# Gate functions as one activation each: x times sigmoid on ScalarE, without VectorE's multiplication

## The chip, the core and the metric

The kernel runs on one NeuronCore of one Trainium2 chip. Its engines are TensorE (PE in the profile, with PEld for its weight loads), VectorE (DVE), ScalarE (ACT), GpSimd (POOL) and SyncE (SP, which starts the DMAs). The program lists the instructions of each engine in an order of its own, and an engine that waits for an operand holds up what is listed behind it. The metric is device time in microseconds, the lower the better.

## What is computed

Chunked attention, then two feed-forward layers, all in float32. The attention output of 4608 tokens with 512 features goes through a layer with a gate and a value branch (d_ff 1536), then through one with a gate alone (d_ff 2048):

```python
def _moe_ref(x, w_gate, w_val, w_out) -> np.ndarray:
    g = x @ w_gate
    silu = g * (1.0 / (1.0 + np.exp(-g)))
    val = x @ w_val
    return (silu * val @ w_out).astype(np.float32)

def _moe2_ref(x, w_in, w_out) -> np.ndarray:
    h = x @ w_in
    g = h * (1.0 / (1.0 + np.exp(-1.702 * h)))
    return (g @ w_out).astype(np.float32)
```

## The kernel before

Matrix products run as three products of a high and a low part each (mm3, lines 249 to 251), so every operand has to be split: ACT or POOL casts the high part, DVE or POOL subtracts it from the value to get the low part (split, line 244, which calls copy and tt). Both layers use seven products for a 2x2 block of products (labels "1" to "7"), with sums and differences of the blocks made on DVE and POOL.

There are four passes over 9 blocks of 512 tokens: two over halves of layer 1's weights, two over halves of layer 2's. In the first pass, attention for the next block (attend, line 464) runs between the products; beside each pass DVE, ACT and POOL also convert the weights of the next one (conv_part, line 323).

In layer 1, group_products (line 579) makes seven products, ACT copies some of them out of PSUM and DVE adds others to them, into tiles c (gate and value beside one another). gated (line 606) then takes Sigmoid of the gate on ACT into h (line 613), multiplies h by the gate and then by the value on DVE (line 616, which is recorded as line 242), and splits h into hh and hl. second (line 623) multiplies these by the output weights.

In layer 2, group_gated (line 632) makes seven products in the order of ORDER[2], "1675243". Almost all of them go through one PSUM bank, ga: the next product waits until ACT has copied the last one out (labels "1", "6", "7", "5") or DVE has added it (labels "2", "4", "3"). gate (line 647) takes Sigmoid with scale 1.702 into a quarter of xr (line 654) and multiplies it by its argument on DVE (line 656). From the four gates of a step DVE makes the combinations (lines 706 to 713), which are split for the seven last products (last_product, line 717). Between two products of ga, PE works on last products of the step before.

The order on each engine isn't the order of the code. Program.emit (line 99) sorts the operations with a list scheduler: each operation has an estimated time (act_us, dve_us, pool_us, GV, YS, OS; 1.3 us for a change of ACT's function table), a due time and its dependences, and at each step the scheduler emits the operation that can start first by these estimates; among those that can start within 0.1 us (DVE) or 0.3 us (others) it takes the one due first. An operation that is taken away therefore changes the order on all engines after it.

Of the kernel before, what the change touches and what calls it, by code (L numbers as in the profile page):

```python
# [12 lines left out]
AF = mybir.ActivationFunctionType  # L13
ALU = mybir.AluOpType
# [55 lines left out]
class Program:  # L70
# [5 lines left out]
    def op(self, eng, us, fn, reads=(), writes=(), prio=0, table=None, near=None):  # L76
        o = Op()
        o.eng, o.us, o.fn, o.prio, o.table, o.near, o.n = eng, us, fn, prio, table, self.slack if near is None and eng not in ('pe', 'dma') else near, len(self.ops)
        deps, follows = set(), set()
        for b in reads:  # L80
            deps.update(next((a.writers for a in b.line() if a.writers), ()))
        for b in writes:
            deps.update(b.users)
            if not b.users:
                if b.prev is not None:
                    deps.update(b.prev.users)
                if b.before is not None and b.before.tile is None:
                    follows.add(b.before.users[0])
        for b in (*reads, *writes):
            for a in b.line():  # L90
                a.users.append(o)
        for b in writes:
            for a in b.line():
                a.writers.append(o)
        o.deps, o.follows = deps, follows - deps
        self.ops.append(o)
        return o
# [44 lines left out]
def attention_two_moe_kernel(ctx: ExitStack, tc: tile.TileContext, q, k, v, wg, wv, wo, wi, wo2, out):  # L142
# [25 lines left out]
    nc = tc.nc  # L168
# [16 lines left out]
    scale = 1.0 / float(D) ** 0.5  # L185
# [18 lines left out]
    op = prog.op  # L204
# [8 lines left out]
    def act_us(n):  # L213
        return (200 + n) / 1.2e3

    def dve_us(n):
        return (148 + n) / 0.96e3

    def pool_us(n):
        return (128 + n) / 0.46e3  # L220
# [10 lines left out]
    def copy(dst, src, n, prio, eng="act", cut=lambda ap: ap, near=None):  # L231
        if eng == "act":
            op("act", act_us(n), lambda: nc.scalar.copy(out=dst.ap, in_=cut(src.ap)), [src], [dst], prio, near=near)  # L233
        elif eng == "pool":
            op("pool", pool_us(0.6 * n), lambda: nc.gpsimd.tensor_copy(dst.ap, cut(src.ap)), [src], [dst], prio)  # L235
        else:
            op("dve", dve_us(n), lambda: nc.vector.tensor_copy(dst.ap, cut(src.ap)), [src], [dst], prio)

    def tt(dst, a, b, by, n, prio, eng="dve", of_a=lambda ap: ap, of_b=lambda ap: ap, near=None):
        e = nc.vector if eng == "dve" else nc.gpsimd  # L240
        op(eng, dve_us(n) if eng == "dve" else pool_us(n),
           lambda: e.tensor_tensor(out=dst.ap, in0=of_a(a.ap), in1=of_b(b.ap), op=by), [a, b], [dst], prio, near=near)  # L242

    def split(hi, lo, src, n, prio, eng="dve", cut=lambda ap: ap, hi_eng="act"):
        copy(hi, src, n, prio, hi_eng, cut)
        tt(lo, src, hi, ALU.subtract, n, prio, eng, of_a=cut, of_b=rd)
# [321 lines left out]
    def product(m, w, x, goes_on, prio, near=None):  # L568

        def fn():  # L570
            for var in range(2):
                for kk in range(2):
                    ks = slice(kk * P, kk * P + P)
                    mm3(m.ap[:, var], w.ap[:, var, 0, ks], w.ap[:, var, 1, ks], x.ap[:, 0, kk], x.ap[:, 1, kk],
                        kk == var == 0 and not goes_on, kk == 1, skip_group_check=True)

        op("pe", GV, fn, [w, x], [m], prio, near=near)
# [28 lines left out]
    def gated(g, c, prio):  # L606

        def of(var):
            return lambda ap: ap[:, :, var]

        for i in (1, 0):
            h = ring["h"].new([P, 2, HT])
            op("act", act_us(512), lambda h=h, i=i: nc.scalar.activation(  # L613
                out=h.ap, in_=of(0)(c[i].ap), func=AF.Sigmoid), [c[i]], [h], prio, "sig")
            for var in range(2):
                tt(h, h, c[i], ALU.mult, 512, prio, of_b=of(var))
            hh = ring["hh"].new([P, BT], F32R)
            hl = ring["hl"].new([P, BT], F32R)
            split(*[Buf(lambda s=s: s.ap.rearrange("p (n t) -> p n t", n=2), s.prev, s.before, s) for s in (hh, hl)],
                  h, 512, prio)  # L620
            yield i, hh, hl
# [10 lines left out]
    def group_gated(g, xs, at, put, early, apart):  # L632


        s1, u2, u3 = [ring["u"].new([P, 2, HT]) for _ in range(3)]
        made = {}
        hs = []

        quarters = []

        def quarter():
            if not quarters:
                c = ring["c"].new([P, 2, 2, HT])
                quarters.extend(c.part(lambda ap, k=k: ap[:, k]) for k in range(2))
            return quarters.pop(0)

        def gate(c, k, prio):
            if apart:
                h = ring["ttte"[k]].new([P, 2, HT])
            else:  # L650
                if not hs:
                    hs.append(ring["xr"].new([P, 4, 2, HT]))
                h = hs[0].part(lambda ap: ap[:, k])
            op("act", act_us(512), lambda: nc.scalar.activation(out=h.ap, in_=c.ap, func=AF.Sigmoid, scale=1.702),  # L654
               [c], [h], prio, "sig")
            tt(h, h, c, ALU.mult, 512, prio)
            return h

        def parts(label, src, prio, eng="dve"):
            made[label] = [ring[t].new([P, 2, HT], F32R) for t in HOMES[label]]  # L660
            split(*made[label], src, 512, prio, eng)

        def follow(label, prio):
            m = bank[label]
            if label == "1":
                copy(s1, m, 512, prio, near=0.3)
            elif label == "6":
                copy(u2, m, 512, prio, near=0.3)
            elif label == "7":
                copy(u3, m, 512, prio, near=0.3)  # L670
                tt(u2, u2, u3, ALU.subtract, 512, prio, "pool")
            elif label == "5":
                c = quarter()
                copy(c, m, 512, prio, near=0.3)
                tt(u2, u2, c, ALU.add, 512, prio, "pool")
                a["22"] = gate(c, 3, prio + 1)
                parts("4", a["22"], prio + 3, "pool")
            elif label == "2":
                c = quarter()
                tt(c, s1, m, ALU.add, 512, prio, near=0.3)  # L680
                a["11"] = gate(c, 0, prio + 1)
                parts("1", a["11"], prio + 2)
            elif label == "4":
                c = quarter()
                tt(c, u3, m, ALU.subtract, 512, prio, near=0.3)
                a["12"] = gate(c, 1, prio + 1)
                parts("2", a["12"], prio + 3)
            else:
                c = quarter()
                tt(c, u2, m, ALU.add, 512, prio, near=0.3)  # L690
                a["21"] = gate(c, 2, prio + 1)

        a = {}
        alone = {"2": "gb", "3": "s", "4": "a"} if early else {}
        z = ring["ga"].new([P, 2, HT])
        bank = {label: ring[alone[label]].new([P, 2, HT]) if label in alone else z for label in ORDER[2]}
        for i, label in enumerate("1263745" if early else ORDER[2]):
            n = ORDER[2].index(label)
            product(bank[label], W[g][n], xs[n], label in "675", at(i), 0.25)
            if label != "3" or not early:  # L700
                follow(label, at(i))
            if i == 6:
                if early:
                    follow("3", at(i))
                prio = at(i)
                tt(a["22"], a["21"], a["22"], ALU.add, 512, prio + 1)
                parts("5", a["22"], prio + 2)
                tt(a["21"], a["11"], a["21"], ALU.subtract, 512, prio + 2)
                tt(a["11"], a["22"], a["11"], ALU.subtract, 512, prio + 2)
                parts("6", a["11"], prio + 3)  # L710
                parts("7", a["21"], prio + 4)
                tt(a["12"], a["12"], a["11"], ALU.subtract, 512, prio + 4)
                parts("3", a["12"], prio + 5)
            put(i)
        return made
# [152 lines left out]
    for p, (layer, gs) in enumerate(passes):  # L868
        jobs = spread(p)
        for b in range(NB):  # L870
            t = start[p][b]
            xs = X.pop((p, b))
            for j, g in enumerate(gs):
# [10 lines left out]
                def at(i, tj=tj, step=step):  # L884
                    return tj + (i + (i > 4)) * step / 8

                if layer == 1:
                    c = group_products(g, xs, at, put, p)
# [106 lines left out]
```

## Time and profile before

| | us |
|---|---|
| median of three runs | 1773.23 |
| lowest and highest run | 1772.24, 1777.48 |
| span of the profiled execution | 1771.6 |
| PE busy | 1702.8 (96%) |
| DVE busy | 1307.8 (74%) |
| ACT busy | 878.3 (50%) |
| POOL busy | 765.7 (43%) |

The span reaches from the first to the last instruction of one profiled execution. The execution's own time isn't given apart from it; the lowest run is 0.6 us above the span, the median 1.6. Instructions are grouped by the line that records them: line 242 is tt, so DVE's multiplications, additions and subtractions all stand under it and are told apart by their tiles (h<-h,c and xr<-xr,c are the gate multiplications, c<-u,ga an addition that empties bank ga, hl<-h,hh a low part). An "idle before" of an engine is put down to the operation that released it.

### The profile page before, as it was taken

To read this page: it belongs to the slowest core of one execution; us is meant where nothing else is said; L and a number is where in the kernel's file an instruction comes from. 1 tells how busy PE (TensorE), PEld (TensorE's weight loads), DVE (VectorE), ACT (ScalarE), POOL (GpSimd) and SP (SyncE) were. 2 spreads that over 40 slices of the span, in tenths; PEclk is the share of its full clock that TensorE was granted. 3 is DMA by queue.
4 is the path that set the end of the run, shared out by engine and by line. 5 is a ranking of instruction groups with operands and counts; after the bars stand their busy time and mean duration, and the time that the engine had idled before them with its cause. 6 is when DMAs were issued, how large, how long until landed. Compare 5 with 4: busy or idle time off the path is not lost.

```text
span 1771.6 us, 36678 instructions
## 1 busy us (share of the span) xinstructions
PE 1702.8 (96%) x14392; PEld 1617.6 (91%) x14392; DVE 1307.8 (74%) x1884; ACT 878.3 (50%) x1534; POOL 765.7 (43%) x762
## 2 busy tenths in 40 slices
PE   6879999999999999999999989999999999999998
PEld 6769988989898999999999989999999999999997
DVE  6888788777876467555555659899887777777777
ACT  5766566666663344333333345555554444444442
POOL 4664456355643145422222225667563133333333
PEclk8889999999999999999999999999999999999999
DMA  6467887788778989877778997888889977776775
GB/s 249 162 220 268 280 280 256 252 300 282 251 256 316 338 280 314 291 262 255 256 250 270 362 354 257 283 273 299 283 285 312 377 264 243 245 238 215 229 224 160
DMA packets 187325, 477.93 MB, mean 270 GB/s; under 512 B 20112, under 2 KB 47760, under 8 KB 187152
## 3 DMA queue, kind: packets, MB, share of 16 engines
q1 hardware_dynamic: 187152, 475.58, 79.0%
q8 instruction: 114, 1.87, 0.4%
q14 instruction: 59, 0.48, 0.1%
HBM read 334.46 MB, written 141.03 MB: 268 GB/s over the span
## 4 chain that ended last, share of the span: by engine, by line
PE 76%; DVE 11%; DMA 5%; issue 2%; POOL 1%; ACT 1%; SPq 0%; POOLq 0%; ACTq 0%; DVEq 0%
PE ga L249 9%; PE ga L251 9%; PE ga L250 9%; PE yb L249 4%; PE ya L250 4%; PE ya L251 4%; PE ya L249 4%; PE yb L251 4%; PE yb L250 4%; PE gb L249 4%; PE gb L251 4%; PE gb L250 4%; DVE xr L242 2%; PE s L249 2%; PE s L250 2%
## 5 line engine op out<-in xcount | busy, mean ns | idle before, releaser
L249 PE MATMUL ga<-x,w 128*128 128x256 f32 x1640 | 472.3, 288 | 26.0 <-DVE c L242 12.3
L250 PE MATMUL ga<-x,w 128*128 128x256 f32 x1640 | 464.5, 283 | 3.0 <-DVE x L242 3.0
L251 PE MATMUL ga<-x,w 128*128 128x256 f32 x1640 | 464.7, 283 | 0.0
L249 PEld LDWEIGHTS ga<-x,w 128*128 128x128 f32 x1640 | 312.1, 190 | 38.5 <-ACT u L233 15.2
L250 PEld LDWEIGHTS ga<-x,w 128*128 128x128 f32 x1640 | 312.1, 190 | 7.6 <-DVE x L242 3.3
L251 PEld LDWEIGHTS ga<-x,w 128*128 128x128 f32 x1640 | 312.0, 190 | 0.0
L233 ACT COPY u<-ga 128x512 f32<-128x512 f32 x231 | 135.4, 586 | 243.9 <-PE ga L251 243.3
L242 DVE TENSOR_TENSOR c<-u,ga 128x512 f32<-128x512 f32 x143 | 97.9, 684 | 120.8 <-PE ga L251 119.8
L242 DVE TENSOR_TENSOR h<-h,c 128x512 f32<-128x512 f32 x216 | 170.6, 807 | 12.6 <-ACT h L613 10.9
L654 ACT ACTIVATE xr<-c 128x512 f32<-128x512 f32 x140 | 87.4, 631 | 139.8 <-DVE c L242 101.7
L249 PE MATMUL gb<-x,w 128*128 128x256 f32 x500 | 142.6, 285 | 2.7 <-DVE c L242 2.7
L251 PE MATMUL gb<-x,w 128*128 128x256 f32 x500 | 141.2, 282 | 0.0
L250 PE MATMUL gb<-x,w 128*128 128x256 f32 x500 | 140.8, 282 | 0.0
L242 DVE TENSOR_TENSOR xr<-xr,c 128x512 f32<-128x512 f32 x140 | 128.4, 924 | 12.9 <-ACT xr L654 12.7
L242 POOL TENSOR_TENSOR u<-u 128x512 f32<-128x512 f32 x36 | 53.9, 1498 | 189.9 <-ACT u L233 188.2
L242 DVE TENSOR_TENSOR c<-u,gb 128x512 f32<-128x512 f32 x125 | 85.3, 682 | 65.9 <-ACT u L233 42.9
L613 ACT ACTIVATE h<-c 128x512 f32<-128x512 f32 x108 | 68.1, 633 | 121.0 <-DVE c L242 120.7
L235 POOL CAST ws<-t 128x256 fp32r<-128x256 f32 x78 | 50.6, 649 | 162.2 <-DVE h L242 65.0
L242 DVE TENSOR_TENSOR xr<-xr 128x512 f32<-128x512 f32 x140 | 111.2, 794 | 1.4
L242 POOL TENSOR_TENSOR k<-xr,q 128x512 fp32r<-128x512 f32 x24 | 41.3, 1720 | 158.1 <-DVE xt L242 69.0
L235 POOL CAST ws<-st 128x256 fp32r<-128x256 f32 x88 | 51.4, 584 | 120.5 <-DMA od_b<-ws 46.8
L249 PEld LDWEIGHTS gb<-x,w 128*128 128x128 f32 x500 | 94.5, 189 | 5.8 <-DVE c L242 3.1
(255 smaller groups left out, 5175.2 us busy)
## 6 DMA issues: line engine op xcount, KB each, us to landing
x<-x_dram SPq DMA_DIRECT2D x189, 512.0 KB, 5.5
o<-od_b SPq DMA_DIRECT2D x126, 512.0 KB, 4.5
o<-od_a SPq DMA_DIRECT2D x102, 512.0 KB, 5.2
x_dram<-x SPq DMA_DIRECT2D x63, 512.0 KB, 4.6
wd_b<-ws SPq DMA_DIRECT2D x56, 256.0 KB, 4.7
od_b<-ws SPq DMA_DIRECT2D x56, 256.0 KB, 4.8
w<-wd_b SPq DMA_DIRECT2D x28, 512.0 KB, 6.4
raw<-in_moe_w_out SPq DMA_DIRECT2D x56, 255.8 KB, 4.5
```

The source lines that it names most:

```text
L233: op("act", act_us(n), lambda: nc.scalar.copy(out=dst.ap, in_=cut(src.ap)), [src], [dst], prio, near=near)
L235: op("pool", pool_us(0.6 * n), lambda: nc.gpsimd.tensor_copy(dst.ap, cut(src.ap)), [src], [dst], prio)
L242: lambda: e.tensor_tensor(out=dst.ap, in0=of_a(a.ap), in1=of_b(b.ap), op=by), [a, b], [dst], prio, near=near)
L249: nc.tensor.matmul(o, ah, bh, start=first, stop=False, **kind)
L250: nc.tensor.matmul(o, ah, bl, start=False, stop=False, **kind)
L251: nc.tensor.matmul(o, al, bh, start=False, stop=last, **kind)
L613: op("act", act_us(512), lambda h=h, i=i: nc.scalar.activation(out=h.ap, in_=of(0)(c[i].ap), func=AF.Sigmoid), [c[i]], [h], prio, "sig")
L654: op("act", act_us(512), lambda: nc.scalar.activation(out=h.ap, in_=c.ap, func=AF.Sigmoid, scale=1.702), [c], [h], prio, "sig")
```

## The change

Layer 1's gate becomes AF.Silu in one activation, and only the multiplication by the value stays. Layer 2's gate becomes AF.Gelu_apprx_sigmoid, and no multiplication stays. The names handed to the planner for the function table change too.

```diff
@@ -611,9 +611,8 @@
         for i in (1, 0):
             h = ring["h"].new([P, 2, HT])
             op("act", act_us(512), lambda h=h, i=i: nc.scalar.activation(
-                out=h.ap, in_=of(0)(c[i].ap), func=AF.Sigmoid), [c[i]], [h], prio, "sig")
-            for var in range(2):
-                tt(h, h, c[i], ALU.mult, 512, prio, of_b=of(var))
+                out=h.ap, in_=of(0)(c[i].ap), func=AF.Silu), [c[i]], [h], prio, "silu")
+            tt(h, h, c[i], ALU.mult, 512, prio, of_b=of(1))
@@ -651,9 +650,8 @@
-            op("act", act_us(512), lambda: nc.scalar.activation(out=h.ap, in_=c.ap, func=AF.Sigmoid, scale=1.702),
-               [c], [h], prio, "sig")
-            tt(h, h, c, ALU.mult, 512, prio)
+            op("act", act_us(512), lambda: nc.scalar.activation(out=h.ap, in_=c.ap, func=AF.Gelu_apprx_sigmoid),
+               [c], [h], prio, "gelu")
             return h
```

The number of instructions on PE, POOL and SP stays; DVE has 252 fewer, ACT one function table load more (43 for 42). What moves shows at two places.

DVE, at the start of layer 2's first pass (at 1057 us in the trace of before), as it stood. c<-u,ga is the addition that empties bank ga, xr<-xr,c the gate multiplication, hl<-xr,hh a low part, raw and xt are low parts of tokens:

```order
L242 TENSOR_TENSOR raw<-xr,raw 128x512
L242 TENSOR_TENSOR xt<-t,xt 128x512
L242 TENSOR_TENSOR xr<-xr,c 128x512 x4
L242 TENSOR_TENSOR c<-u,ga 128x512
L242 TENSOR_TENSOR hl<-xr,hh 128x512 x2
L242 TENSOR_TENSOR c<-u,ga 128x512
```

The same place now:

```order
L242 TENSOR_TENSOR xt<-t,xt 128x512
L242 TENSOR_TENSOR raw<-xr,raw 128x512
L242 TENSOR_TENSOR c<-u,ga 128x512
L242 TENSOR_TENSOR hl<-xr,hh 128x512
L242 TENSOR_TENSOR c<-u,ga 128x512
L242 TENSOR_TENSOR hl<-xr,hh 128x512
```

Four multiplications ahead of the addition are gone, and the second addition now stands between the two low parts.

ACT, in one step near the end of the second pass of layer 2, before. u and c receive the copies of products "1", "6", "7" and "5" out of bank ga in this order; h, v, q and xt receive the high parts of the combinations of the step before; e receives a sum of the output:

```order
L233 COPY u_21377<-ga_21352 128x512
L233 COPY u_21409<-ga_21352 128x512
L233 CAST h_21418<-xr_21261 128x512
L233 CAST v_21433<-xr_21261 128x512
L233 CAST q_21437<-xr_21261 128x512
L233 COPY u_21445<-ga_21352 128x512
L233 CAST xt_21455<-xr_21261 128x512
L233 COPY e_21474<-ya_21185 128x512
```

Such a step now:

```order
L233 COPY u_20658<-ga_20636 128x512
L233 CAST h_20681<-xr_20529 128x512
L233 CAST v_20690<-xr_20529 128x512
L233 CAST q_20702<-xr_20529 128x512
L233 COPY u_20710<-ga_20636 128x512
L233 CAST xt_20720<-xr_20529 128x512
L233 COPY e_20738<-ya_20369 128x512
L233 COPY u_20748<-ga_20636 128x512
L233 COPY c_20767<-ga_20636 128x512
```

The casts now stand ahead of the copies of products "6" and "7", and the copies of "7" and "5" stand side by side. On PE, the number of last products between two products of bank ga changes with it: in the second pass of layer 2 all 125 gaps held two; now 82 hold two, 26 hold one, 8 three and 9 four. The gaps with one stand behind products "7" and "5", those with three or four behind "6".

## Rows read from the trace of the kernel before

**Rows 1.** Page, part 1: busy us (share of the span) xinstructions.

```profile
PE 1702.8 (96%) x14392; PEld 1617.6 (91%) x14392; DVE 1307.8 (74%) x1884; ACT 878.3 (50%) x1534; POOL 765.7 (43%) x762
```

**Rows 2.** Busy time by stretch; first the length, last PEclk, DMA share, GB/s.

```profile
45.00:120.00 75.00, 57.54 (x596) 50.90 (x597) 62.75 (x96) 53.33 (x105) 49.65 (x52) 0.84 0.50 164
120.00:600.00 480.00, 470.65 (x4465) 429.79 (x4464) 369.79 (x566) 284.60 (x480) 229.12 (x263) 0.99 0.82 280
610.00:1010.00 400.00, 398.98 (x2763) 371.33 (x2763) 236.30 (x349) 147.69 (x263) 133.43 (x125) 1.00 0.83 280
1025.00:1110.00 85.00, 78.17 (x632) 75.97 (x631) 66.48 (x93) 44.68 (x81) 37.28 (x33) 1.00 0.83 295
1110.00:1210.00 100.00, 93.30 (x758) 91.95 (x759) 87.75 (x125) 55.32 (x100) 65.08 (x68) 0.98 0.85 280
1210.00:1410.00 200.00, 195.86 (x1632) 194.36 (x1631) 164.35 (x225) 99.22 (x175) 101.36 (x104) 1.00 0.89 310
1410.00:1760.00 350.00, 348.29 (x2930) 347.91 (x2928) 272.93 (x364) 158.19 (x270) 121.38 (x84) 1.00 0.72 234
```

**Rows 3.** Groups by line (count; busy, mean ns; idle before); x68 covers 1025:1395.

```profile
L242 DVE TENSOR_TENSOR h<-h,c 128x512 f32<-128x512 f32 x216 | 170.6, 807 | 12.6 <-ACT h L613 10.9
L242 DVE TENSOR_TENSOR xr<-xr,c 128x512 f32<-128x512 f32 x140 | 128.4, 924 | 12.9 <-ACT xr L654 12.7
...
L242 DVE TENSOR_TENSOR xr<-xr,c 128x512 f32<-128x512 f32 x68 | 60.5, 904 | 0.4 <-ACT xr L654 0.2
...
L233 ACT COPY u<-ga 128x512 f32<-128x512 f32 x231 | 135.4, 586 | 243.9 <-PE ga L251 243.3
L654 ACT ACTIVATE xr<-c 128x512 f32<-128x512 f32 x140 | 87.4, 631 | 139.8 <-DVE c L242 101.7 <-DVE xt L242 34.3 <-DVE raw L242 3.1
...
L613 ACT ACT_TABLE_LOAD x21 | 26.9, 1283 | 0.4
```

**Rows 4.** PE's waits from 1000 to 1360: us in total, times, longest us.

```profile
PE ga L249 <- DVE c L242: 12.3, 8, 3.0
PE ga L249 <- ACT u L233: 4.5, 8, 0.7
```

**Rows 5.** Order of time: start, us, engine, operation [idle before]; DVE and PE.

```profile
1059.32 2.50 DVE L242 TENSOR_TENSOR xr<-xr,c 128x512 f32<-128x512 f32 x4
1061.73 0.68 DVE L242 TENSOR_TENSOR c<-u,ga 128x512 f32<-128x512 f32 x1
...
1062.47 0.39 PE L249 MATMUL ga<-x,w 128*128 128x256 f32 x1 [1.66 <-DVE c L242]
...
1112.08 0.67 DVE L242 TENSOR_TENSOR c<-u,ga 128x512 f32<-128x512 f32 x1
...
1112.81 0.58 PE L249 MATMUL ga<-x,w 128*128 128x256 f32 x1 [2.97 <-DVE c L242]
```

**Rows 6.** Order of time, PE: first matmuls of products of bank ga.

```profile
1149.57 0.39 PE L249 MATMUL ga<-x,w 128*128 128x256 f32 x1 [0.26 <-ACT u L233]
...
1151.93 0.39 PE L249 MATMUL ga<-x,w 128*128 128x256 f32 x1
...
1170.99 0.28 PE L249 MATMUL ga<-x,w 128*128 128x256 f32 x1
...
1173.25 0.39 PE L249 MATMUL ga<-x,w 128*128 128x256 f32 x1
...
1176.34 0.39 PE L249 MATMUL ga<-x,w 128*128 128x256 f32 x1
...
1194.26 0.28 PE L249 MATMUL ga<-x,w 128*128 128x256 f32 x1
...
1198.24 0.38 PE L249 MATMUL ga<-x,w 128*128 128x256 f32 x1 [1.66 <-DVE c L242]
```

**Rows 7.** Order of time in layer 1's first pass, DVE and PE.

```profile
59.50 3.04 DVE L242 TENSOR_TENSOR h<-h,c 128x512 f32<-128x512 f32 x3
...
65.79 0.79 PE L249 MATMUL ya<-hh,o 128*128 128x512 f32 x1 [3.45 <-ACT hh L233]
...
365.25 4.11 DVE L242 TENSOR_TENSOR h<-h,c 128x512 f32<-128x512 f32 x4 [0.33 <-ACT h L613]
```

## The prediction

> **What bounds the kernel now.** I read the shares by engine first, then the table of stretches, then PE's waits, then the order of time around single waits. TensorE (PE) is busy 96% of the span [rows 1], so a cheaper VectorE (DVE) is worth only what PE now loses to it. The stretches [rows 2] say where that is. From 1410 to 1760 us (second pass of layer 2) PE starts 2930 matmuls in 350 us, 119.5 ns each, with 1.7 us idle: nothing to win. From 610 to 1010 us (second pass of layer 1) it idles 1.0 us in 400: nothing to win either. The first pass of layer 2, 1025 to 1410 us, is different: at 119.5 ns its 632, 758 and 1632 matmuls need 75.5, 90.6 and 195.0 us of 85, 100 and 200, so 9.5 + 9.4 + 5.0 = 23.9 us are lost, 17.7 us of them plain idle time. There DVE is busy 66.5 of 85, 87.8 of 100 and 164.4 of 200 us. The first pass of layer 1 (120 to 600) idles 9.4 us, and the stretch before it, 45 to 120, idles 17.5 us at a mean granted clock of 0.84 of full speed. So about 45 us are open in all, over half of them where the clock or attention matter as much as DVE does.
>
> In layer 2's first pass, 12.3 us of PE's idle time are eight waits for DVE's addition that empties bank ga, 4.5 us are eight waits for ScalarE's (ACT's) copy out of it [rows 4]. The two examples show the same thing: DVE works without a pause, and the addition that PE waits for stands behind other work. At 1059.32 four gate multiplications (2.50 us) run, only then the addition at 1061.73, and PE goes on at 1062.47 after 1.66 us idle; the addition at 1112.08 lets PE go on at 1112.81 after 2.97 us [rows 5].
>
> **What the change removes.** In layer 1, 108 of 216 multiplications of 807 ns: 87.2 us of DVE. In layer 2, 140 of 924 ns, 129.4 us by that product (128.4 in the row), and four into other tiles, some 3 us more [rows 3]. DVE's 1307.8 us falls by about 219 us. None of it is saved as such.
>
> *Layer 2, first pass.* 68 of those multiplications lie there, at 904 ns: 60.5 us [rows 3], 3.6 us in each step of four gates. That is more than the longest of the eight waits, 2.97 us, and at the start of the pass the four multiplications ahead of the addition are just gone from the queue (order of DVE). A wait also costs the restart: the starts at 1194.26 and 1198.24, one product and one last product apart (18 matmuls, 2.15 us), lie 3.98 us apart, 1.83 lost for 1.66 idle [rows 6]. So the eight are worth 12.3 to some 15 us. What stays: ACT's copies and their 4.5 us, and weight conversion may move into the places that come free. I take 11 us; ends 4 (a third of the waits go) and 15.
>
> *Layer 1, first pass, 120 to 600.* Four multiplications at a stretch take 4.11 us at 365.25 [rows 7]; two stay. Other waits there are behind attention and conversion, which stay. Of 9.4 us I take 3; ends 8 us gained and 4 us lost, since the planner also moves attention against the last products.
>
> *45 to 120.* At 59.50 three multiplications take 3.04 us, and PE waits 3.45 us at 65.79 for the high half of the gate [rows 7]. Two of the four there are gone, 2.0 us, and two more at the next gate. I take 2.5; ends 4 gained and 3 lost (the clock, not this queue, may decide).
>
> **What it keeps.** One ACTIVATE of 128x512 per gate stays, with another function. No row shows the new functions; Sigmoid takes 631 ns (L654) and a plain copy 586 [rows 3]. I take Sigmoid's time, so nothing is added; the ends are the copy (0.05 us less per gate) and a second pass over the tile (0.63 more), which is a rival below. The Trainium skill ("ScalarE: Activation LUTs", section "Step-by-step: what each stage is for") says that every function costs the same per element; by it the sum stays as it is.
>
> *Function tables.* 42 loads before, 43 in the changed order: layer 1's function alternates with attention's Exp as Sigmoid did, and one load is new, at the first gate of layer 2. A load is 1283 ns [rows 3]. ACT is in order, so the copies out of PSUM behind it wait with it; uncovered that is 1.3 us, hidden it is 0. I take 1. The same page ("What ACT_TABLE_LOAD costs") adds a drain of about 1.38 us to each load; the 21 loads of the row have 0.4 us of idle time before them in total, so the trace does not show it here. By the page this term would be 2.7 us and the sum 1.7 us worse.
>
> **What it moves.** The planner places work by its own estimates; with a gate 0.82 us shorter it deals out PE's work anew. The gaps between two products of bank ga, counted in the order of PE: in the second pass of layer 2 all 125 held two last products; now 82 hold two, 26 one, and 17 three or four. The thin ones follow products "7" and "5", which ACT copies out. In a gap PE can't start the next product until that copy is done. The old first pass has such gaps with ACT on time: starts at 1149.57 and 1151.93, 2.36 us for 2.15 of work, 0.21 lost; and at 1170.99, 1173.25 and 1176.34, where 42 matmuls (5.02 us) take 5.35, 0.33 lost with the slower product behind the gap [rows 6]. 26 times 0.11 (the first half of that, 2.26 for 2.15) to 0.33 is 2.9 to 8.6 us. I take 0.23, 6 us **lost** in a stretch that now loses nothing. In layer 1's second pass four banks take turns, so its moved products wait for nothing; I take 0. The DMAs are the same, one for one, on SP's queue.
>
> **Sum**, against the profiled span of 1771.6 us: -11 (layer 2, first pass) - 3 (layer 1, first pass) - 2.5 (start) + 1 (table) + 6 (thin gaps) = -9.5, so 1762.1. The median of the runs shown, 1773.23, is 1.6 above that span; I add it: **1763.7 us**, 0.5% less.
>
> **Rivals.**
> *The relief is hidden.* PE's waits pass from DVE to the chain that remains: product, addition, activation, cast, subtraction, with single-bank turnaround and conversion filling DVE again. For it: ACT's copies already end 4.5 us of the waits, and the planner refills free DVE time. Against it: DVE is 78 to 88% busy there [rows 2] and four multiplications stand right ahead of a waited-for addition. Then only about a third of the gains is kept (4 + 1 + 1), against 6 + 1: 1773 + 1 = 1774. Chance 0.16.
> *ACT's queue makes the thin gaps dear (slower).* In the new order casts of the combinations (lines 243 to 246, tiles v, q, xt) stand ahead of the copies of products "6" and "7". If DVE delivers those combinations late, the copy waits behind the cast and PE behind the copy. The price is that of the one thin gap with a late partner, 1.83 us [rows 6], in half of the 26: 13 x 1.6 = 21 us beside the 6, so 1763.7 + 21 = 1785. It decides from the point at which a combination comes later than the end of product "7". For it: the copies stand one behind the other with a cast between. Against: DVE does 3.6 us less per step. Chance 0.08.
> *The activation is two passes long.* 0.63 us more for 248 gates; the path from addition to product then shortens by only 0.2 to 0.3 us, DVE's relief stays. Half of the gains, (11 + 3 + 2.5)/2 = 8 against 7: 1772. Chance 0.05.
> *More comes free*: all eight waits, and the start with its clock: 15 + 8 + 4 gained, 2.9 lost: 24 us, 1749. Chance 0.11.
>
> **How the numbers follow.** The forecast has 0.60. About 0.3% (5.3 us) is what a measurement of this kernel can tell from no change, so faster means under 1767.9 and slower above 1778.5. The forecast case splits 0.53 faster, 0.06 same, 0.01 slower by its terms' ends; the hidden relief 0.03, 0.12, 0.01; the long activation 0.01, 0.04, 0; more comes free is faster, ACT's queue slower. In all 0.68, 0.22 and 0.10. Low end: all gains at their best, 1749. High end: gains at 4 + 0 + 0, losses at 8.6 and 1.3 gives 1779; the ACT-queue case lies beyond it.
>
> **What would show it.** Right: DVE busy near 1089 us in all; the waits of PE's ga for DVE in layer 2's first pass under 3 us; matmuls in the second pass of layer 2 slower than 119.5 ns with PE idle some us on ACT's copies; activations near 631 ns and 43 table loads. Wrong: DVE waits of PE as before (hidden relief); single waits over 1 us on ACT's copy of "7" (ACT's queue); gates near 1.2 us; or a start that is longer at a lower clock, which would eat a third of the gain.

## The result, and the profile after

The changed kernel takes 1754.18 us in the median (1750.8 to 1755.69), the kernel before 1774.1 beside it: ratio 0.9871, 95% interval 0.9852 to 0.989. The medians are 19.9 us apart; the ratio, which the interval belongs to, says 1.3% less, or some 23 us. Every ratio below is to runs of the kernel before on the same chip, and its median differs from chip to chip (1774 to 1778 us), so kernels that ran on different chips are compared by their ratios and by their stages. The direction was forecast, and the time lies inside the range (1749 to 1779), but the forecast gain was 9.5 us: it was less than half of what came.

The first lines of the page of the changed kernel (busy us, share of the span, number of instructions):

```profile
span 1751.4 us, 36463 instructions
...
PE 1704.3 (97%) x14392; PEld 1617.2 (92%) x14392; DVE 1111.5 (63%) x1632; ACT 882.3 (50%) x1535; POOL 735.2 (42%) x762
```

Against [rows 1], DVE has 196 us less (1307.8 to 1111.5) and PE's busy time is the same. The span is 20.2 us shorter; the execution that was profiled took 1753.21 us, 1.8 above its span.

Busy time by stretch, with the bounds moved to where the same work now lies (columns as in [rows 2]):

```profile
45.00:120.00 75.00, 61.43 (x642) 55.00 (x642) 65.20 (x102) 56.81 (x112) 53.30 (x56) 0.89 0.56 186
120.00:588.00 468.00, 463.40 (x4417) 424.10 (x4416) 329.44 (x518) 287.42 (x483) 233.56 (x274) 1.00 0.85 289
1013.00:1098.00 85.00, 80.94 (x658) 79.00 (x657) 59.48 (x87) 50.05 (x90) 37.86 (x36) 1.00 0.88 312
1098.00:1198.00 100.00, 99.75 (x837) 99.38 (x836) 78.45 (x108) 55.18 (x99) 62.39 (x72) 1.00 0.89 305
1198.00:1363.00 165.00, 164.84 (x1380) 163.93 (x1379) 112.71 (x159) 85.86 (x150) 84.06 (x93) 1.00 0.91 311
1363.00:1740.00 377.00, 375.31 (x3097) 369.67 (x3096) 212.00 (x309) 168.97 (x285) 117.62 (x87) 1.00 0.74 236
```

In layer 2's first pass PE starts 837 matmuls in the 100 us where it started 758 in [rows 2], and idles 0.3 us where it idled 6.7. The last row, the second pass of layer 2, is the other side: 3097 matmuls in 377 us are 121.7 ns each, where [rows 2] had 119.5.

PE's waits from 1000 to 1360 us (us in total, times, longest), against [rows 4]:

```profile
PE ga L249 <- ACT c L233: 1.6, 3, 0.7
PE ga L249 <- DVE c L242: 1.4, 3, 1.0
PE ga L249 <- ACT u L233: 1.4, 2, 0.7
```

The waits for DVE's addition fell from 12.3 us to 1.4.

**A table by stage.** To set kernels side by side whose stages start at other times, I count PE's work in units: a product of seven (12 matmuls, 1.43 us), a last product of layer 2 (6, 0.715), a second product of layer 1 (3, 0.695), an attention block (1.08) and a transposition (0.36), each as long as the traces show it where PE doesn't wait. A stage lasts from the first matmul of one product to that of another; what it lasts beyond the sum of its units is "lost". The stages begin at products 1, 22, 190, 379 and 505 of 630: "start" is up to the end of the first block, then the rest of layer 1's first pass, its second pass, and layer 2's two passes, the last one up to the last products at its end. All of it is worked out from the traces, one execution each.

| lost us | start | rest, L1 pass 1 | L1 pass 2 | L2 pass 1 | L2 pass 2 |
|---|---|---|---|---|---|
| before | 38.3 | 23.2 | 1.4 | 24.4 | 3.2 |
| changed | 31.1 | 18.3 | 1.4 | 7.3 | 11.3 |
| after_again | 30.8 | 15.7 | 1.3 | 7.8 | 9.2 |
| a_old_order | 36.4 | 25.4 | -0.1 | 11.3 | 3.5 |
| b_off_chain | 38.7 | 22.7 | 0.1 | 22.4 | 13.7 |
| b2_off_chain | 37.4 | 23.6 | 0.9 | 25.9 | 5.0 |
| c_layer1 | 30.3 | 17.9 | 2.3 | 21.5 | 4.7 |
| d_layer2 | 37.5 | 28.3 | 0.4 | 8.1 | 11.1 |
| k_hold_layer1 | 36.5 | 25.2 | 0.9 | 8.8 | 9.0 |
| e_new_order_old_work | 37.7 | 39.4 | 4.7 | 35.7 | 16.8 |
| j_even_gaps | 31.6 | 16.6 | 2.1 | 6.7 | 3.3 |
| j_again | 32.0 | 19.3 | 1.6 | 6.7 | 3.5 |

The second column is good to about 5 us: before and d_layer2 have the same order and the same work there and read 23.2 and 28.3. In the two pairs that are one kernel traced twice (changed and after_again, j_even_gaps and j_again) the others repeat to about 2 us; in layer 2's first pass before, b_off_chain, b2_off_chain and c_layer1, where DVE has its full work there, read 21.5 to 25.9.

Where an experiment below holds an order, the traces bear it out: PE, POOL and SP run the same instructions in the same order in a_old_order, b_off_chain and b2_off_chain as in the kernel before, and in e_new_order_old_work as in the changed kernel. k_hold_layer1 has the order of d_layer2 on these engines and on ACT too.

### The profile page after: what moved, and what is told of

It is laid out like the page before. It is cut to its first block, busy times and chain, and to the rows that moved or that the text cites. A ratio compares the mean times of both kernels' runs of the same rounds, so it can differ in the third digit from the quotient of the medians.

```text
span 1751.4 us, 36463 instructions
## 1 busy us (share of the span) xinstructions
PE 1704.3 (97%) x14392; PEld 1617.2 (92%) x14392; DVE 1111.5 (63%) x1632; ACT 882.3 (50%) x1535; POOL 735.2 (42%) x762
## 4 chain that ended last, share of the span: by engine, by line
PE 86%; DVE 5%; ACT 2%; issue 2%; DMA 1%; POOL 0%; POOLq 0%; ACTq 0%; DVEq 0%
PE ga L249 11%; PE ga L251 10%; PE ga L250 10%; PE yb L249 4%; PE ya L250 4%; PE ya L249 4%; PE ya L251 4%; PE yb L251 4%; PE yb L250 4%; PE gb L249 4%; PE gb L251 4%; PE gb L250 4%; PE s L249 2%; PE s L251 2%; PE s L250 2%
## 5 line engine op out<-in xcount | busy, mean ns | idle before, releaser
L249 PE MATMUL ga<-x,w 128*128 128x256 f32 x1640 | 472.9, 288 | 10.9 <-ACT u L233 3.9
L235 POOL CAST ws<-t 128x256 fp32r<-128x256 f32 x78 | 41.0, 526 | 193.7 <-DMA wd_b<-ws 85.5
L242 DVE TENSOR_TENSOR xr<-xr 128x512 f32<-128x512 f32 x140 | 117.4, 839 | 5.4 <-ACT xr L653 3.1
L242 POOL TENSOR_TENSOR k<-xr,q 128x512 fp32r<-128x512 f32 x24 | 37.5, 1564 | 173.8 <-ACT q L233 64.7
L242 DVE TENSOR_TENSOR hl<-h,hh 128x512 fp32r<-128x512 f32 x108 | 92.0, 872 | 17.0 <-ACT hh L233 16.8
L249 PEld LDWEIGHTS gb<-x,w 128*128 128x128 f32 x500 | 95.4, 191 | 4.3 <-DVE c L242 1.7
L242 POOL TENSOR_TENSOR u<-u 128x512 f32<-128x512 f32 x36 | 48.7, 1352 | 117.7 <-ACT u L233 117.7
L242 POOL TENSOR_TENSOR yv<-yv,e 128x512 f32<-128x512 f32 x18 | 23.2, 1288 | 177.2 <-ACT e L233 115.9
L250 PEld LDWEIGHTS gb<-x,w 128*128 128x128 f32 x500 | 95.5, 191 | 2.0
```

The costliest lines, as they stand in the source:

```text
L249: nc.tensor.matmul(o, ah, bh, start=first, stop=False, **kind)
L250: nc.tensor.matmul(o, ah, bl, start=False, stop=False, **kind)
```

## The experiments

After the result I held the **queue theory**: PE waited because other work stood ahead of the additions in DVE's queue, and a shorter queue makes those waits go whatever the order. Rivals: the **order theory** (the planner's new order made the gain) and the **chain theory** (the shorter way from a gate to its last products made it).

### Old order without the multiplications

The planner goes on reckoning with a multiplication, and nothing is emitted for it:

```diff
+            op("dve", dve_us(512), lambda: None, [h, c[i]], [h], prio)
             tt(h, h, c[i], ALU.mult, 512, prio, of_b=of(1))
...
+            op("dve", dve_us(512), lambda: None, [h, c], [h], prio)
             return h
```

> The changed kernel's activations, without the dropped multiplications, but in the order of the kernel before: the planner still reckons with a multiplication of 0.69 us after each gate, and nothing is emitted for it. PE, POOL and SP have the very order of before; DVE has that order less the multiplications. Queue theory (PE waited because work stood ahead of the additions in DVE's queue; shorter queue, fewer waits, in either order): the loss in layer 2's first pass falls from 24 us to about 7 as in the changed kernel, the two layer 1 stretches gain as there, and the second pass of layer 2 loses 3 us instead of 11, since all its gaps hold two last products again: 1746 us (1743 to 1750), 8 less than the changed kernel. Order theory (the planner's new order made the gain, the multiplications as such little): layer 2's first pass still loses over 15 us, in all 1762 to 1774.

Measured: 1759.81 us, ratio 0.9903 (0.9882 to 0.9923). The changed kernel has 0.9871, so this one is not 8 us faster but, if anything, slower (the two intervals just meet); the stages lose 76.5 us in all where the changed kernel loses 69.4. The time lies between what the two theories said. Its stretches, at the bounds of [rows 2] but for the last:

```profile
1025.00:1110.00 85.00, 78.61 (x637) 76.52 (x636) 57.26 (x82) 45.74 (x84) 35.25 (x32) 1.00 0.85 301
1110.00:1210.00 100.00, 98.97 (x829) 98.42 (x828) 81.62 (x113) 56.58 (x104) 65.27 (x73) 1.00 0.90 306
1210.00:1410.00 200.00, 199.50 (x1673) 198.65 (x1672) 137.35 (x189) 97.97 (x177) 90.45 (x100) 1.00 0.90 317
1410.00:1745.00 335.00, 333.93 (x2810) 333.75 (x2809) 204.14 (x276) 147.46 (x259) 117.92 (x82) 1.00 0.71 229
```

In layer 2's first pass the shorter queue does most of it in the old order: from 1110 on PE idles 1.5 us in 300 where it idled 10.8, and the pass loses 11.3 us for 24.4. The new order brings another 3 to 4 (7.3 and 7.8 us lost in two executions). In the second pass the old order loses nothing (119.2 ns per matmul), so what the changed kernel loses there on top (8 us in one execution, 6 in the other) is the new order's. But in layer 1 the shorter queue alone gains next to nothing: 36.4 and 25.4 us lost for 38.3 and 23.2.

### The same work on DVE, beside the chain

```diff
+            op("dve", dve_us(512), lambda: nc.vector.tensor_tensor(
+                out=c.ap, in0=c.ap, in1=c.ap, op=ALU.mult), [h, c], [h], prio)
```

and the same on the gate's half of c in layer 1.

> As a_old_order, but where the multiplication stood DVE multiplies the gate's argument by itself, in place (nothing reads that result). DVE has as much work as before, at the same places, but the chain from activation to the high part no longer goes through it. Queue theory: back to the kernel before, 1774 us (1770 to 1777), loss in layer 2's first pass 22 to 25 us. Chain theory (the gain came from the shorter way from a gate to its last products): like a_old_order, about 1746 to 1752.

Measured: 1784.95 us, ratio 1.0039 (1.0021 to 1.0056). The experiment had a fault of its own in the second pass of layer 2 (13.7 us lost). The group of these multiplications, whose result nobody reads, there:

```profile
L657 DVE TENSOR_TENSOR c<-c 128x512 f32<-128x512 f32 x72 | 59.8, 830 | 28.0 <-POOL u L242 28.0
```

DVE waits 28 us for GpSimd, which still reads the tile that is overwritten; the multiplication that was dropped wrote elsewhere and had no such wait. So it was made again with another target:

```diff
+            aside = quarters[0] if k == 3 else c
+            op("dve", dve_us(512), lambda: nc.vector.tensor_tensor(
+                out=aside.ap, in0=c.ap, in1=c.ap, op=ALU.mult), [h, c], [h], prio)
```

> As b_off_chain, which had put a new wait for GpSimd into layer 2 (DVE overwrote a tile that GpSimd still read, 28 us of waiting): now DVE's idle multiplication writes to the other half of the tile where GpSimd reads the first. DVE's work is that of before at the same places, the chain from a gate to its last products goes past it. Queue theory: 1774 to 1777 us, loss in layer 2's first pass 22 to 25 us, 3 us in its second. Chain theory: the loss in layer 2's first pass near the 11 us of a_old_order, in all 1758 to 1764.

Measured: 1778.23 us, ratio 1.0005 (0.9985 to 1.0025): the kernel before, to within the interval. The half tile aside already holds the next gate's argument in some steps, so those gates are evaluated on other values; the instructions are the same ones. PE's waits from 1000 to 1390 us:

```profile
PE ga L249 <- DVE c L242: 12.0, 7, 3.0
PE ga L249 <- ACT u L233: 3.5, 5, 0.7
```

These are [rows 4] over again (seven waits for eight, 12.0 us for 12.3), though no last product waits for a multiplication any more. The chain theory falls for layer 2's first pass, and the queue theory holds there: DVE's time at these places is what PE waited for.

### The new order with the old work

```diff
-            op("act", act_us(512), lambda: nc.scalar.activation(out=h.ap, in_=c.ap, func=AF.Gelu_apprx_sigmoid),
-               [c], [h], prio, "gelu")
+            def old_gate():
+                nc.scalar.activation(out=h.ap, in_=c.ap, func=AF.Sigmoid, scale=1.702)
+                nc.vector.tensor_tensor(out=h.ap, in0=h.ap, in1=c.ap, op=ALU.mult)
+
+            op("act", act_us(512), old_gate, [c], [h], prio, "gelu")
```

and the same in layer 1.

> The changed kernel's order of PE, POOL and SP, but the old work: Sigmoid, and right behind it in the order the multiplication on DVE, which the planner does not reckon with. Queue theory: DVE's waits come back in layer 2's first pass (loss 22 us or more) and the thin gaps of the second pass cost 8 us beside, since their copies also wait longer: 1782 us (1775 to 1795). Order theory: most of the gain stays, 1754 to 1764.

Measured: 1819.1 us, ratio 1.0246 (1.0224 to 1.0268), 37 us beyond what the queue theory said. DVE's groups of it say why (the columns of [rows 3]):

```profile
L658 DVE TENSOR_TENSOR xr<-xr,c 128x512 f32<-128x512 f32 x140 | 122.4, 874 | 96.1 <-ACT xr L657 91.2
L615 DVE TENSOR_TENSOR h<-h,c 128x512 f32<-128x512 f32 x108 | 87.0, 806 | 56.5 <-ACT h L614 54.5
```

A multiplication listed right behind its activation makes DVE stand and wait for ACT, 91 and 55 us, where [rows 3] have 12.7 and 10.9. So this kernel is more than the new order with the old work, and its 45 us can't be put down to the order alone. Every stage but the start is worse than before, but whether the new order would gain anything with the old work, if DVE didn't stand, isn't shown.

### Each layer alone

Layer 2's gate alone changed:

> Only layer 2's gate changed; layer 1 keeps Sigmoid and two multiplications. Queue theory: the 12 us that the two layer 1 stretches gained are gone, layer 2 keeps its gain of 17 in the first pass and its loss of 8 in the second: 1774 - 9 = 1765 us (1761 to 1769). Order theory, where layer 1's new order gave the start its gain: the same 1765. If the two layers help one another through what is carried over, under 1760.

Measured: 1765.05 us, ratio 0.9943 (0.9925 to 0.9961), as expected; the losses of layer 2 are those of the changed kernel.

Layer 1's gate alone changed:

> Only layer 1's gate changed; layer 2 keeps Sigmoid and its multiplication, and the second pass of layer 2 keeps two last products in every gap. If the parts add up, layer 1's 12 us are gained and layer 2's losses stay at 24 and 3 us: 1762 us (1759 to 1766), ratio to the kernel before 0.993. If layer 1's gain needs layer 2's change too, 1772 or more.

Measured: 1760.39 us, ratio 0.9904 (0.9879 to 0.993), as expected: 30.3 and 17.9 us lost in layer 1's first pass, and layer 2 as before. The parts add up within the intervals: 0.57% and 0.96% make 1.5%, the changed kernel has 1.3%.

### Layer 1 in the old order, layer 2 in the new

The first line alone of the diff of a_old_order.

> The changed kernel, where the planner still reckons with one multiplication of 0.69 us after each gate of layer 1 (nothing is emitted): layer 1 runs in the order of the kernel before, without its first multiplications; layer 2's order is that of d_layer2. If layer 1's 12 us came from the new order, as a_old_order says (start 36.4 us lost for 38.3 of before and 31.1 of the changed kernel; the rest of the pass 25.4 for 23.2 and 18.3), nearly all of it is missing: about 1764 us, no better than d_layer2 within 3 us. If the shorter queue alone does it, 1754.

Measured: 1763.93 us, ratio 0.9923 (0.9897 to 0.9948), the 1764 of the order reading. Beside d_layer2 it has 108 multiplications less in layer 1 and loses 36.5 and 25.2 us there instead of 37.5 and 28.3; with the new order as well, the changed kernel loses 31.1 and 18.3. The other kernels say the same: with layer 1 in the old order they lose 36.4 to 38.7 and 22.7 to 28.3 us, in the new order and with the shorter gates 30.3 to 32.0 and 15.7 to 19.3.

PE's waits for ACT's copies out of bank ga, from 40 to 600 us, in the kernel before, in a_old_order and in the changed kernel (us in total, times, longest):

```profile
PE ga L249 <- ACT u L233: 7.2, 4, 2.2
PE ga L249 <- ACT u L233: 7.7, 5, 3.3
PE ga L249 <- ACT u L233: 2.5, 2, 1.4
```

Three of them lie in the rest of the pass, behind 129 us: 5.9 us before and 5.8 in a_old_order (6.8 in k_hold_layer1, 6.9 in d_layer2), none in the changed kernel and in after_again, 0.8 in c_layer1. So these waits stay when the multiplications alone go, and they go with the new order. They are of the size of what the rest of the pass gained; what in the new order ends them was not followed further.

Why the shorter queue gives next to nothing at the start shows at the first gate; the other gates were not looked at one by one. ACT in a_old_order, in order of time (start, us, engine, operation, idle before):

```profile
58.89 1.15 ACT L613 ACTIVATE h<-c 128x512 f32<-128x512 f32 x2
61.34 0.76 ACT L328 ACTIVATE t<-w,offset 128x512 f32<-128x512 int16 x1 [1.30 <-POOL st L242]
62.14 0.77 ACT L330 ACTIVATE w<-w,offset 128x512 f32<-128x512 int16 x1
...
65.06 0.60 ACT L233 CAST hh<-h 128x512 fp32r<-128x512 f32 x1
```

and DVE in it:

```profile
59.99 0.73 DVE L242 TENSOR_TENSOR h<-h,c 128x512 f32<-128x512 f32 x1
62.99 0.69 DVE L333 SCALAR_TENSOR_TENSOR t<-t,w 128x512 int32<-128x512 f32 x1 [2.28 <-POOL w L242]
```

The multiplication by the value is done at 60.7, but the cast to the high part stands behind weight conversion in ACT's queue, which waits for GpSimd, and starts at 65.06. DVE, with less to do, now stands 2.28 us for GpSimd. In the changed kernel the cast starts at 64.92, no earlier; there the planner has put an attention block into the gap:

```profile
62.48 1.15 PE L483 MATMUL s<-k,q 64*64 64x64 f32 x32
65.58 0.50 PE L249 MATMUL ya<-hh,o 128*128 128x512 f32 x1 [1.95 <-ACT hh L233]
```

In a_old_order the same wait is idle throughout:

```profile
65.72 0.49 PE L249 MATMUL ya<-hh,o 128*128 128x512 f32 x1 [2.91 <-ACT hh L233]
```

### Even gaps in the second pass of layer 2

```diff
+            if cur[0] == 3 and k in (0, 1):
+                op("dve", 0.6, lambda: None, [h, c], [h], prio)
             return h
```

cur[0] is the number of the pass, counted from 0; the lines that set it are left out here.

> The changed kernel, with one addition for the planner alone: in the second pass of layer 2 it reckons with 0.6 us more on DVE after two of the four gates, and nothing is emitted for that. The order up to that pass is the changed kernel's; in that pass 121 of 125 gaps between products of bank ga hold two last products, 3 hold one (26 before). If the thin gaps are what the changed kernel loses there (11.3 us lost, 3.2 in the kernel before), the loss falls to 4 to 5 us and the time to 1747 us (1744 to 1750), ratio to the kernel before about 0.983. If the loss lies elsewhere (transfers at the end, copies behind casts), the time stays at 1754.

Measured: 1744.11 us, ratio 0.9823 (0.9797 to 0.9849). The second pass of layer 2 loses 3.3 us. Its stretch:

```profile
1361.00:1734.00 373.00, 370.92 (x3109) 369.55 (x3107) 234.39 (x310) 165.02 (x285) 122.79 (x87) 1.00 0.73 240
```

3109 matmuls in 373 us are 120.0 ns each, for 121.7 in the changed kernel. To be sure that this isn't a difference of chips, both ran once more side by side.

> The changed kernel once more, beside j_again on one chip, so that the two can be set against the same runs of the kernel before. Ratio 0.985 to 0.989; stages as first seen: 7 us lost in layer 2's first pass, 11 in its second.

> j_even_gaps once more, beside after_again. If the thin gaps are worth what the stages said, it is 7 to 9 us below after_again: ratio 0.981 to 0.985, 3 to 4 us lost in the second pass of layer 2. If the first difference was one of chips, the two are within 3 us.

Measured: after_again 1751.13 us, ratio 0.9862 (0.9838 to 0.9887); j_again 1745.83 us, ratio 0.9825 (0.9805 to 0.9844). The difference is 5.3 us, a little under what was expected, and all four runs of j_again (1744.16 to 1746.47) lie below all four of after_again (1749.07 to 1754.43); the stage gives 9.2 to 3.5. This is the version that beats both kernels.

How a thin gap costs, in the changed kernel. PE's first matmuls of three products in a row, with one last product in each gap (18 matmuls, 2.15 us):

```profile
1492.44 0.28 PE L249 MATMUL ga<-x,w 128*128 128x256 f32 x1
...
1494.76 0.39 PE L249 MATMUL ga<-x,w 128*128 128x256 f32 x1
...
1497.13 0.39 PE L249 MATMUL ga<-x,w 128*128 128x256 f32 x1
```

and ACT's copies between them:

```profile
1494.12 0.59 ACT L233 COPY u<-ga 128x512 f32<-128x512 f32 x1 [1.60 <-PE ga L251]
1496.49 0.59 ACT L233 COPY c<-ga 128x512 f32<-128x512 f32 x1 [1.78 <-PE ga L251]
```

ACT stands ready before each copy (at all 26 thin gaps it had been idle for at least 1.3 us), so nothing holds it up; from the end of one product over the copy to the start of the next is just longer than one last product. The starts lie 2.32 and 2.37 us apart for 2.15 of work. The 26 thin gaps of that pass cost 0.16 to 0.23 us each, 4.9 in all, and the gaps behind them another 1.3 together.

## Why the prediction was right or wrong

**What bounds the kernel**: right. All that was won lies where PE waited, and the two stages named as without any gain (second passes) gave none. Stage by stage the sum was 2.5 + 3 + 11 - 6 = 10.5 us, less 1 for the table; it came to 7.2 + 4.8 + 17.1 - 8.1 = 21.0.

**DVE's relief**: 219 us forecast, 196 measured. Some of the instructions that stay got slower, for a reason that no run here isolates: the combinations xr<-xr from 794 to 839 ns and the low parts hl<-h,hh from 789 to 872.

**Layer 2, first pass**: the first step that failed. Taken at 11 us, at best 15; it gave 17.1 (24.4 to 7.3). The mechanism was right, and b2_off_chain shows it: give DVE the time back beside the chain, and the waits are there again (seven, 12.0 us). The sum failed because it counted only PE's waits for DVE, 12.3 us and their restarts. The shorter queue gave 13.1 (a_old_order), above the 11 but inside the ends, and the planner's new order another 3 to 4, for which there was no term. The waits for ACT's copy that I wrote off as staying fell too, from 4.5 us to 3.0 with both kinds of copy.

**Layer 1, first pass and start**: 3 + 2.5 us forecast, 4.8 + 7.2 measured, above the best end at the start. This is the second step that failed, and here the mechanism was wrong. At the start I put the gain down to two multiplications fewer ahead of the high part. But [rows 7] show DVE and PE alone, and the prediction doesn't take in ACT's queue, which in the kernel before reads at that place:

```profile
64.70 0.53 ACT L330 ACTIVATE raw<-raw,offset 128x256 f32<-128x256 int16 x1
65.14 0.60 ACT L233 CAST hh<-h 128x512 fp32r<-128x512 f32 x1
```

DVE was through with its three multiplications at 62.54 [rows 7]; the cast stood behind weight conversion in ACT's queue all along. k_hold_layer1 and a_old_order, without those multiplications but in the old order, gain about 2 us at the start and nothing that can be told in the rest. With the same work, the new order makes the difference. The clock doesn't: from 45 to 120 us the granted clock was 0.84 of full speed before and 0.89 now, but d_layer2 and b2_off_chain, in the old order, had 0.88 and lost 37.5 and 37.4 us at the start. I had the order in the prediction: the planner moves attention against the last products. I gave it a loss as an end and no gain of its own.

**Both terms miss the same thing**: the planner's order is a cost or a gain of the change like its work. It was priced in one place only, where it lost. Whether this order would gain anything without the shorter gates is open: e_new_order_old_work is slower than the kernel before, but it also makes DVE stand for ACT.

**Thin gaps**: right, and where they were forecast. 6 us taken, 2.9 to 8.6 the ends; 6.2 measured at the gaps (4.9 + 1.3), 8.1 in the stage. Of the other 1.9 us, about 1 is the units, which are a little too long (the 125 gaps of the kernel before read -1.1 us by them), and the rest lies behind the last product of bank ga, where the three waits for weights are 3.9 us in all in both kernels. The sign that I had named for it, PE idle on ACT's copies, didn't come: PE idles 1.7 us in its row, as it did before [rows 2], and the loss shows in the distance between starts alone.

**Function tables**: 43 loads of 1283 ns, as forecast. The new one stands ahead of the first gate of layer 2; whether its 1 us was paid can't be told from the 7.3 us lost in that pass.

**The activations**: 632 ns for x times sigmoid in layer 1, 631 in layer 2, against Sigmoid's 631: no second pass. The groups of the changed kernel:

```profile
L653 ACT ACTIVATE xr<-c 128x512 f32<-128x512 f32 x140 | 88.3, 631 | 135.1 <-DVE c L242 128.2 <-DVE xt L242 5.4 <-DVE raw L242 0.8
L613 ACT ACTIVATE h<-c 128x512 f32<-128x512 f32 x108 | 67.9, 632 | 118.6 <-DVE c L242 118.0
L613 ACT ACT_TABLE_LOAD x21 | 26.9, 1283 | 0.4
```

The Trainium skill ("ScalarE: Activation LUTs", section "Step-by-step: what each stage is for") says that all functions cost the same per element; these traces agree (631 to 633 ns in the groups of 108 and 140, for Sigmoid, Silu and Gelu_apprx_sigmoid). Of the drain that the Trainium skill (the same page, section "What ACT_TABLE_LOAD costs") adds to each load, this trace shows nothing, as before: 0.4 us idle before 21 loads.

**The rivals**: hidden relief and the long activation didn't come about. ACT's queue didn't make the gaps dear: its copies at the thin gaps found ACT idle. "More comes free", 24 us at a chance of 0.11, is the nearest to the truth in size, but not for its reason: it counted waits and clock, not order.

## What to carry to other kernels

Where a planner orders the work by its estimates, dropping an instruction makes two changes, the work and the order; hold the planner's estimate fixed to measure the first alone, and price the second at each place where the order differs, for gain as well as loss. Where the operation that is waited for stands behind other work in its engine's list, as DVE's additions did in layer 2's first pass, the wait is worth the time of that work, not of the chain that the operand comes through. An instruction that gets its operand sooner gains nothing if it is listed behind something slower, like the cast at 65 us, so look at the queue of the engine that comes next too.

## What the runs showed of the hardware

Not expected, and in these kernels' own sizes: a bank that is emptied by a copy of 590 ns and filled again by the next product needs more than one last product of 0.715 us between: 0.16 to 0.23 us are lost with one, 0.82 to 0.93 with none (four cases in layer 2's first pass of the changed kernel), nothing with two. The product after a pause is slower, too: 1.53 us for 1.43. And in b_off_chain DVE waited 28.0 us over 72 instructions for GpSimd, which still read the tile that they overwrite.
